# A gated mix of linear attention and a squared-relu block: TensorE in source order, keys of 448 columns, logits on VectorE

## The chip, the cores and the metric

The kernel runs on one core of a Trainium2 chip. The metric is the device time of one execution in microseconds (us); lower is better. A core has a matrix engine (TensorE, PE in the profile; its weight loads are PEld), three elementwise engines (VectorE = DVE, ScalarE = ACT, GpSimd = POOL), and SyncE (SP), which here issues nearly all DMAs. Each engine takes its own instructions in the order in which they stand in its queue, and waits on semaphores for the others.

## The reference

All tensors are fp32: 2048 tokens, model width 448, 16 heads of 28, hidden width 1792.

```python
def _A_ref(x, wqkv, wo):                       # linear attention
    q, k, v = split_heads(x @ wqkv)
    phi = lambda t: where(t > 0, t + 1, exp(t)) + 1e-6
    pq, pk = phi(q), phi(k)
    kv = einsum("bhsd,bhse->bhde", pk, v)
    z  = einsum("bhsd->bhd", pk)
    num = einsum("bhqd,bhde->bhqe", pq, kv)
    den = einsum("bhqd,bhd->bhq", pq, z)[..., None] + 1e-6
    return merge_heads(num / den) @ wo
def _B_ref(x, w1, b1, w2, b2):                 # squared relu block
    h = maximum(x @ w1 + b1, 0)
    return (h * h) @ w2 + b2
g = sigmoid((x * gate_w).sum(-1, keepdims=True))
out = g * _A_ref(x, ...) + (1 - g) * _B_ref(x, ...)
```

## The kernel before

Every fp32 operand of a product is split into a high and a low part of a rounded fp32 type; a product is then three matmuls (high × high, high × low, low × high). The width of 448 is cut into three chunks of 128 rows and a last one of 64, whose high and low parts share one chunk, so a full contraction over the width is 3 + 3 + 3 + 2 = 11 matmuls. The splits are elementwise work: ScalarE makes the high part (`split_hi`), VectorE the low part by a subtraction (`split_lo`); GpSimd takes a few.

The tokens are cut into four blocks `b` of 512, and the 1792 hidden columns into 14 tiles `f` of 128. The names in the profile:

- `up(b,f)`: 11 matmuls of 512 columns into `h_ps` (line 213). `hidden`: relu and square on ScalarE (`hr`, lines 217 and 218), then high and low part on VectorE (`hh`, `hl`). `down(b,f)`: 12 matmuls of 448 columns into the four `o_ps` tiles (line 242).
- `keys(t)`: 11 matmuls into `k_ps` for each of 16 token tiles `t`; 450 columns, since the gate's weights stand twice beside the 448 key columns, and a copy on VectorE (line 280) takes the logit from there. Then phi (`e`, `r`), the split (`ph`, `pl`), and `nh`, `nl`, the split of the raw `xn` tile.
- `gram(b,c)`: the products of keys and x, `g_ps`, summed in `gsum`.
- `kv_product`: `kv_ps`, then `kv_h`, `kv_l`. `m_product(j)`: for each of four groups of heads, three matmuls of the split `wo` (`woh`, `wol`) with kv into `m_ps`; ScalarE and VectorE evacuate it into the tile `m`, and five DMAs of GpSimd's queue bring it to `m_s`.
- `queries(b,c)`: `q_ps`, 11 matmuls (7 for c = 3). For c = 3 ScalarE copies the result (`qv`), eight small DMAs on SP swap its rows (`qr`), and VectorE adds the two (`join`). `after` is phi (exp on ScalarE, lines 261 and 262 on VectorE) and the sum `ds` for the denominators.
- `denominators(b)`: `d_ps`, from the split `dh`, `dl` of `ds`; VectorE makes `rec` from it. `scaled(b,c)`: the queries times `rec`, split (`qh`, `ql`). `attention(b,i)`: 11 matmuls of 448 columns with `m_s` (`a_ps`), added to `part`. `finish(b,i)`: the output tile, and its store.

Pass 1 goes through the four blocks with f = 0 to 6, and keeps the partial sums of `down` in `part`; the keys of a block and its `gram` go along. Pass 2 goes through the blocks in the order 3, 0, 1, 2 with f = 7 to 13; `kv_product` and `m_product` are in its first block, with the queries of block 3 between them, and in each block the queries of the next are made. PSUM has three pools: four tiles for `o_ps`, two for `h_ps`, and two (`ms_p`) shared by everything else: `k_ps`, `g_ps`, `kv_ps`, `m_ps`, `q_ps`, `d_ps`, `a_ps`, and two of the first four `h_ps` tiles. A new tile there waits until the one that had its bank has been read.

The order on every engine is set by a scheduler, which orders the program's instructions. Steps that read a result later are put on a list (`todo`), which `run_todo` empties a step on.

Of the kernel before, what the change touches and what calls it, by code (L numbers as in the profile page):

```python
# [7 lines left out]
F = mybir.dt.float32  # L8
# [22 lines left out]
def gated_mix_kernel(ctx: ExitStack, tc: tile.TileContext, xt, xn, wk, wq, wv, wo, w1a, w1b, w2, b1, b2, hmask,  # L31
# [4 lines left out]
    keep = ctx.enter_context(tc.tile_pool(name="keep", bufs=1))  # L36

# [122 lines left out]
    warm = keep.tile([P, 400], mybir.dt.bfloat16, name="warm")[:, :256]  # L160
# [42 lines left out]
    def up_chunk(ps, b, f, c):  # L203
        h, fl = divmod(f, NH)
        g, i = divmod(fl, 4)
        w, cols = w1_s[h, g], slice(i * P, (i + 1) * P)
        xh, xl = xs[b]
        if c < 3:
            terms = [(w[:, c, cols], xh[:, c]), (w[:, c, cols], xl[:, c]), (w[:, 4 + c, cols], xh[:, c])]
        else:  # L210
            terms = [(w[:, 3, cols], xh[:, 3]), (w[:, 3, cols], xl[:, 3])]
        for n, (a, m) in enumerate(terms):
            pe.matmul(ps, a, m, start=(c == 0 and n == 0), stop=(c == 3 and n == 1))  # L213

    def hidden(ps, b, f):
        r = slot([P, TB], F, f"hr{b}_{f}")
        act.activation(r, ps, AF.Relu, bias=b1_s[:, f:f + 1])  # L217
        act.activation(r, r, AF.Square)  # L218
        h = slot([P, TB], R, f"hh{b}_{f}")
        lo = slot([P, TB], R, f"hl{b}_{f}")  # L220
        split_hi(dve, h, r)
        split_lo(dve, lo, r, h)
        hs[f] = (h, lo)

    def up(b, f):
# [3 lines left out]
        hidden(ps, b, f)  # L229
# [34 lines left out]
    def keys(t):  # L264
        b, i = divmod(t, 4)
        ps = ms_p.tile([P, 512], F, name=f"k_ps{t}", tag="ms")
        products(ps[:, :D + 2], [term for c in range(4)
                                 for term in terms_x(*xs[b], slice(i * P, (i + 1) * P), wk_s, slice(0, D + 2), c)])
# [9 lines left out]
        def after():  # L278
            phi(ps[:, :D], e, r, p)
            dve.tensor_copy(logit[:, t:t + 1], ps[:, D:D + 1])  # L280
# [12 lines left out]
            pend[t] = (ph, pl, nh, nl)  # L293
# [19 lines left out]
    wq_s = keep.tile([P, 7, TB], R, name="wq_s")  # L313
# [72 lines left out]
    def m_product(j):  # L386
        wh, wl = wo_s.pop(j)
        ps = ms_p.tile([P, 512], F, name=f"m_ps{j}", tag="ms")
        products(ps[:, :D], [(kv[0][:, j], wh), (kv[0][:, j], wl), (kv[1][:, j], wh)])
        m = late.tile([P, 2, D], R, name=f"m{j}", tag="m", bufs=1)  # L390

        def after():
            split_hi(act, m[:, 0], ps[:, :D])
            split_lo(dve, m[:, 1], ps[:, :D], m[:, 0])

            p = j * 32
            for c in range(3):
                pool.dma_start(out=m_s[p:p + 32, c::4, :D][:, :2], in_=m[c * 32:c * 32 + 32])
            pool.dma_start(out=m_s[p:p + 16, 3, :D], in_=m[96:112, 0])
            pool.dma_start(out=m_s[p + 16:p + 32, 3, :D], in_=m[112:, 1])  # L400
        return [after]
# [4 lines left out]
    def queries(b, c):  # L406
# [25 lines left out]
        def swap():  # L432
# [4 lines left out]
            return [join]  # L437
# [30 lines left out]
    def attention(b, i):  # L468
# [13 lines left out]

    todo = []
# [10 lines left out]
    for c in range(4):  # L494
        if c == 0:
            split_x(0, 0, 0, TB // 2)
            split_w1(0, 0, 0, hi_eng=dve)
            split_x(0, 0, TB // 2, TB)
# [3 lines left out]
        for f in range(4):  # L502
            up_chunk(first[f], 0, f, c)
    for f in range(2):
        hidden(first[f], 0, f)
    split_w2(0)
    split_w2(1)
    for f in range(2, 4):
        hidden(first[f], 0, f)

    wkm = keep.tile([P, 3632], R, name="wk_s", tag="wkm", bufs=1)
    wk_s = wkm[:, :7 * TB].rearrange("p (c n) -> p c n", c=7)

    load_xn(0)
# [15 lines left out]
    for c in range(4):  # L530
        split_w1(0, 1, c)
# [25 lines left out]
    todo += gram(0, 0)  # L557
    split_x(1, 2)
    down(0, 5)
    run_todo()  # L560
    todo += gram(0, 1)
    split_x(1, 3)

    for b in range(1, NB):
        for f in range(NH):
            run_todo()
            up(b, f)
            if f == 0:
                down(b - 1, NH - 1)
                half_done(b - 1)  # L570
                if b == 1:
                    todo += gram(0, 2)
                    run_todo()
                    todo += gram(0, 3)
                    run_todo()
# [48 lines left out]
    for n, b in enumerate(order):  # L624
        then = order[n + 1] if n + 1 < NB else None
        for f in range(NF - NH, NF):
            fl = f - NH
            run_todo()
            up(b, f)
# [6 lines left out]
            else:  # L636
                down(order[n - 1], NF - 1)
                for i in range(4):
                    finish(order[n - 1], i)
            if n == 0:  # L640
                if fl < 4:
                    todo += queries(b, (3, 0, 1, 2)[fl])
                if fl == 0:
# [5 lines left out]
                    m_s = keep.tile([P, 3632], R, name="m_s", tag="wkm", bufs=1)  # L649
                    m_s = m_s[:, :7 * D].rearrange("p (c n) -> p c n", c=7)  # L650
                    for j in range(2):
                        load_wo(j)
                if fl == 1:
                    for c in range(4):
                        split_w1(1, 1, c)
                if fl in (1, 2):
                    for j in range(2 * fl - 2, 2 * fl):
                        split_wo(j)
                        todo += m_product(j)
                    if fl == 1:  # L660
                        for j in range(2, 4):
                            load_wo(j)
# [10 lines left out]
                if fl == 6:  # L673
                    for i in range(4):
                        attention(b, i)
            else:
                if fl == 0:
                    todo += denominators(b)
                if fl == 1:
                    for c in range(4):  # L680
                        scaled(b, c)
                if 2 <= fl < 6:
                    attention(b, fl - 2)
            if then is not None:
# [8 lines left out]
                if n == 0 and fl in (5, 6):  # L693
                    for c in ((3, 0), (1, 2))[fl - 5]:
# [57 lines left out]
```

## Time and profile before

| | |
|---|---|
| median of 3 runs | 442.16 us (442.0 to 442.78) |
| profiled execution | 441.92 us, span 440.1 |
| granted clock of TensorE | 1.000 |
| TensorE busy | 432.9 us (98%), 2054 matmuls |
| VectorE, ScalarE, GpSimd busy | 268.0 (61%), 172.7 (39%), 58.5 (13%) |

The span is what the profile records from first to last instruction. A row of groups gives busy time, then the mean of one in ns, then the engine's idle time ahead of them with what ended most of it (`<-`). A row of the timeline or of the chain begins with start and duration in us. Matmuls overlap: a record of 0.39 us follows the one before it by 0.23, so a start-to-start distance tells more than a duration.

### The profile page before, as it was taken

To read this page: it belongs to the slowest core of one execution; us is meant where nothing else is said; L and a number is where in the kernel's file an instruction comes from. 1 tells how busy PE (TensorE), PEld (TensorE's weight loads), DVE (VectorE), ACT (ScalarE), POOL (GpSimd) and SP (SyncE) were. 2 spreads that over 40 slices of the span, in tenths; PEclk is the share of its full clock that TensorE was granted. 3 is DMA by queue.
4 is the path that set the end of the run, shared out by engine and by line. 5 is a ranking of instruction groups with operands and counts; after the bars stand their busy time and mean duration, and the time that the engine had idled before them with its cause. 6 is when DMAs were issued, how large, how long until landed. Compare 5 with 4: busy or idle time off the path is not lost.

```text
span 440.1 us, 5482 instructions
## 1 busy us (share of the span) xinstructions
PE 432.9 (98%) x2054; PEld 380.7 (87%) x2054; DVE 268.0 (61%) x452; ACT 172.7 (39%) x298; POOL 58.5 (13%) x76
## 2 busy tenths in 40 slices
PE   9999999999999999999999989999999999999996
PEld 6798898899888889898988868888888898888895
DVE  5958436552587427573467668788454984549423
ACT  5955235331355114451344334335322453234321
POOL 0233124210252005420002420000000000000000
PEclk9999999999999999999999999999999999999999
DMA  7652201021031210333146311040100501002002
GB/s 264 188 174 69 89 13 57 24 66 47 24 118 31 67 45 1 110 102 82 54 123 151 73 38 24 1 147 33 25 0 0 181 0 26 0 0 85 1 1 83
DMA packets 18315, 28.77 MB, mean 65 GB/s; under 512 B 2880, under 2 KB 12784, under 8 KB 18288
## 3 DMA queue, kind: packets, MB, share of 16 engines
q1 hardware_dynamic: 17072, 26.81, 19.9%
q0 software_dynamic: 1216, 1.61, 1.9%
q8 instruction: 16, 0.26, 0.3%
q14 instruction: 11, 0.09, 0.1%
HBM read 22.09 MB, written 3.67 MB: 59 GB/s over the span
## 4 chain that ended last, share of the span: by engine, by line
PE 91%; DVE 3%; DMA 2%; ACT 2%; issue 1%; SPq 0%; DVEq 0%; ACTq 0%
PE o_ps L242 30%; PE h_ps L213 28%; PE q_ps L77 8%; PE a_ps L77 8%; PE g_ps L77 8%; PE k_ps L77 7%; DMA wkr<-in_wk 1%; DMA xr<-in_xt 1%; PE kv_ps L364 1%; ACT hr L217 1%; PE m_ps L77 1%; DVE wk_s L65 0%; DVE hh L62 0%; DVE r L261 0%; DVE r L262 0%
## 5 line engine op out<-in xcount | busy, mean ns | idle before, releaser
L213 PE MATMUL h_ps<-xh,w 128*128 128x512 f32 x392 | 126.9, 392 | 0.1
L242 PE MATMUL o_ps<-w,hh 128*128 128x448 f32 x448 | 125.5, 363 | 0.7 <-DVE hh L62 0.7
L242 PEld LDWEIGHTS o_ps<-w,hh 128*128 128x128 f32 x448 | 83.8, 188 | 10.2 <-DVE hh L62 1.4
L213 PE MATMUL h_ps<-xl,w 128*128 128x512 f32 x224 | 87.5, 391 | 0.0
L213 PEld LDWEIGHTS h_ps<-xh,w 128*128 128x128 f32 x392 | 73.5, 188 | 15.4 <-ACT xh L58 0.4
L242 PE MATMUL o_ps<-w,hl 128*128 128x448 f32 x224 | 79.6, 363 | 0.0
L217 ACT ACTIVATE hr<-h_ps,b_s 128x512 f32<-128x512 f32 x56 | 38.3, 683 | 96.9 <-PE h_ps L213 89.8
L62 DVE CAST hh<-hr 128x512 fp32r<-128x512 f32 x56 | 25.3, 452 | 40.4 <-ACT hr L218 40.0
L213 PEld LDWEIGHTS h_ps<-xl,w 128*128 128x128 f32 x224 | 42.1, 188 | 8.3 <-DVE xl L65 0.4
L242 PEld LDWEIGHTS o_ps<-w,hl 128*128 128x128 f32 x224 | 42.0, 188 | 2.9 <-DVE hl L65 0.2
L65 DVE TENSOR_TENSOR hl<-hr,hh 128x512 fp32r<-128x512 f32 x56 | 41.1, 734 | 2.2
L218 ACT ACTIVATE hr<-hr 128x512 f32<-128x512 f32 x56 | 35.3, 630 | 1.3
L77 PE MATMUL k_ps<-wk_s,xh 128*128 128x450 f32 x112 | 33.7, 367 | 0.0
L77 PE MATMUL q_ps<-xh,wq_s 128*128 128x512 f32 x100 | 33.0, 390 | 0.0
L77 PE MATMUL a_ps<-m_s,qh 128*128 128x448 f32 x112 | 32.2, 362 | 0.0
L65 POOL TENSOR_TENSOR nl<-xnr,nh 128x384 fp32r<-128x384 f32 x16 | 18.2, 1139 | 94.2 <-ACT nh L58 94.2
L286 POOL TENSOR_TENSOR ksum<-ksum,r 128x448 f32<-128x448 f32 x15 | 19.3, 1284 | 52.1 <-DVE r L262 52.1
L481 DVE SCALAR_TENSOR_TENSOR part<-part,gate,u 128x448 f32<-128x448 f32 x16 | 10.9, 683 | 24.9 <-ACT u L480 24.9
L480 ACT ACTIVATE u<-a_ps,gate 128x448 f32<-128x448 f32 x16 | 10.2, 635 | 37.2 <-PE a_ps L77 37.2
L261 DVE TENSOR_SCALAR r<-k_ps 128x448 f32<-128x448 f32 x16 | 10.0, 623 | 23.7 <-ACT e L260 21.7
L77 PE MATMUL k_ps<-wk_s,xl 128*128 128x450 f32 x64 | 23.6, 369 | 0.0
L77 PE MATMUL g_ps<-pl,nh 128*128 128x448 f32 x64 | 23.3, 364 | 0.3 <-DVE pl L65 0.3
(104 smaller groups left out, 562.0 us busy)
## 6 DMA issues: line engine op xcount, KB each, us to landing
xr<-in_xt SPq DMA_DIRECT2D x27, 256.0 KB, 3.2
xnr<-in_xn SPq DMA_DIRECT2D x16, 224.0 KB, 2.6
out<-out SPq DMA_DIRECT2D x16, 224.0 KB, 2.0
w2r<-in_w SPq DMA_DIRECT2D x14, 224.0 KB, 2.9
w1r<-in_w1a SPq DMA_DIRECT2D x8, 256.0 KB, 2.8
w1r<-in_w1b SPq DMA_DIRECT2D x8, 192.0 KB, 2.9
m_s<-m POOLq DMA_DIRECT2D x12, 112.0 KB, 2.7
wqr<-in_wq SPq DMA_DIRECT2D x4, 256.0 KB, 3.0
```

Of the source, the lines that this page charges most:

```text
L62: eng.tensor_copy(hi, src)
L65: eng.tensor_tensor(lo, src, f32(hi), op=ALU.subtract)
L77: pe.matmul(out_ps, a, b, start=(i == 0), stop=(i == n - 1))
L213: pe.matmul(ps, a, m, start=(c == 0 and n == 0), stop=(c == 3 and n == 1))
L217: act.activation(r, ps, AF.Relu, bias=b1_s[:, f:f + 1])
L218: act.activation(r, r, AF.Square)
L242: pe.matmul(o_ps[i][:, :D], a, m, start=(f % NH == 0 and n == 0), stop=(f % NH == NH - 1 and n == 2))
L261: dve.tensor_scalar(r, ps, 0.0, 1e-6, op0=ALU.max, op1=ALU.add)
L286: pool.tensor_tensor(ksum, ksum, p, op=ALU.add)
L364: pe.matmul(kv_ps[:JE, js], wv_s[c][:, js], gsum[c][:, js], start=(c == 0), stop=(c == 3))
L480: act.activation(u, ps[:, :D], AF.Copy, scale=gate[:, 0, t:t + 1])
L481: dve.scalar_tensor_tensor(part[t], part[t], gate[:, 1, t:t + 1], u, op0=ALU.mult, op1=ALU.add)
```

## The change

TensorE's instructions now keep the order of the source; the other engines are still ordered by the scheduler. The source is rearranged for it. In the head, x is loaded ahead of w1, and the first contraction runs term by term over four up tiles; 15 instead of 18 warming matmuls; wk is split ahead of the first hidden tiles, and w1's second group is loaded right behind wk and split between them. The first and the last hidden tile are made in halves (`parts`). Keys have 448 columns; the logit is a VectorE instruction over the raw `xn` tile and a broadcast copy of the gate's weights (`gw_s`), with an accumulated sum. `gram(0,·)` comes later, `m_product` is one per step, evacuated at once, `join` a step later, the attention of block 3 goes into the next block, `scaled` and `attention` of later blocks a step back.

```diff
-    for _ in range(18):
+    for _ in range(15):
...
+    for c in range(4):
+        load_w1(0, 1, c)
...
-        products(ps[:, :D + 2], [term for c in range(4)
-                                 for term in terms_x(*xs[b], slice(i * P, (i + 1) * P), wk_s, slice(0, D + 2), c)])
+        products(ps[:, :D], [term for c in range(4)
+                             for term in terms_x(*xs[b], slice(i * P, (i + 1) * P), wk_s, slice(0, D), c)])
...
-            dve.tensor_copy(logit[:, t:t + 1], ps[:, D:D + 1])
...
+            dve.scalar_tensor_tensor(e, raw, 1.0, gw_s, op0=ALU.mult, op1=ALU.mult, accum_out=logit[:, t:t + 1])
...
-        def after():
-            split_hi(act, m[:, 0], ps[:, :D])
-            split_lo(dve, m[:, 1], ps[:, :D], m[:, 0])
...
+        split_hi(act, m[:, 0], ps[:, :D])
+        split_lo(dve, m[:, 1], ps[:, :D], m[:, 0])
...
-            return [join]
+            return [lambda: [join]]
...
+    ctx.enter_context(tc.manual_schedule(engines={pe.engine}))
...
+        if c == 0:
+            for n in range(3):
+                for f in range(4):
+                    up_chunk(first[f], 0, f, c, n)
...
+    for c in range(4):
+        split_w(wk_s, c, wk_raw[c], act, dve)
+    hidden(first[0], 0, 0, 2)
+    hidden(first[1], 0, 1)
+    hidden(first[2], 0, 2)
+    for c in range(4):
+        split_w1(0, 1, c)
+    hidden(first[3], 0, 3)
...
-    todo += gram(0, 0)
     split_x(1, 2)
     down(0, 5)
-    run_todo()
-    todo += gram(0, 1)
+    todo += gram(0, 0)
...
-            up(b, f)
+            up(b, f, 2 if then is None and f == NF - 1 else 1)
...
+                    if n == 1:
+                        attention(order[0], i)
                     finish(order[n - 1], i)
             if n == 0:
+                if 1 <= fl < 5:
+                    m_product(fl - 1)
...
-                if fl in (1, 2):
-                    for j in range(2 * fl - 2, 2 * fl):
-                        split_wo(j)
-                        todo += m_product(j)
...
+                if 1 <= fl < 4:
+                    split_wo(fl)
...
-                if fl == 6:
-                    for i in range(4):
-                        attention(b, i)
...
-                if fl == 1:
-                    for c in range(4):
-                        scaled(b, c)
-                if 2 <= fl < 6:
-                    attention(b, fl - 2)
+                if 1 <= fl < 3:
+                    scaled(b, 2 * fl - 2)
+                    scaled(b, 2 * fl - 1)
+                if 3 <= fl:
+                    attention(b, fl - 3)
...
+    down(last, NF - 2, range(3))
     for i in range(4):
-        for f in (NF - 2, NF - 1):
-            down(last, f, [i])
+        if i == 3:
+            down(last, NF - 2, [i])
+        down(last, NF - 1, [i])
         finish(last, i)
```

How the instructions move is seen in the order of each engine's queue (name of the output, then the inputs; the numbers only tell tiles of one name apart). First ScalarE in the head, from the first hidden tile on; `h_ps0_2` is the third up tile, whose bank keys(0) takes. Before:

```order
L217 ACTIVATE hr0_0_231<-h_ps0_0_161,b1_s_115 128x512
L218 ACTIVATE hr0_0_231<-hr0_0_231 128x512
L217 ACTIVATE hr0_1_238<-h_ps0_1_162,b1_s_115 128x512
L218 ACTIVATE hr0_1_238<-hr0_1_238 128x512
L217 ACTIVATE hr0_2_251<-h_ps0_2_163,b1_s_115 128x512
```

Now:

```order
L233 ACTIVATE hr0_0_253<-h_ps0_0_168,b1_s_127 128x256 x2
L234 ACTIVATE hr0_0_253<-hr0_0_253 128x256 x2
L59 ACTIVATE w1_01_278<-w1r010_146 128x384
L233 ACTIVATE hr0_1_264<-h_ps0_1_169,b1_s_127 128x512
L59 ACTIVATE w1_01_278<-w1r011_148 128x384
L234 ACTIVATE hr0_1_264<-hr0_1_264 128x512
L59 ACTIVATE w1_01_278<-w1r012_150 128x384
L59 ACTIVATE w1_01_278<-w1r013_152 128x384
L233 ACTIVATE hr0_2_271<-h_ps0_2_170,b1_s_127 128x512
```

The four casts of w1's second group (`w1_01`) have moved ahead of the relu of the third up tile.

Second, ScalarE in the first block of pass 2, behind the evacuation of kv. Before:

```order
L58 ACTIVATE kv_h_2036<-kv_raw_2034 112x4x112
L434 COPY qv3_2008<-q_ps3_3_1998 128x512
L217 ACTIVATE hr3_8_2082<-h_ps3_8_2070,b1_s_115 128x512
L58 ACTIVATE w2_12_2152<-w2r12_2052 128x448
L218 ACTIVATE hr3_8_2082<-hr3_8_2082 128x512
L58 ACTIVATE xh0_2159<-xr0_0_2057 128x512
```

Now:

```order
L59 ACTIVATE kv_h_2040<-kv_raw_2038 112x4x112
L59 ACTIVATE woh0_2056<-wor0_2052 112x448
L59 ACTIVATE m0_2117<-m_ps0_2113 128x448
L446 COPY qv3_2012<-q_ps3_3_2002 128x512
L233 ACTIVATE hr3_8_2090<-h_ps3_8_2078,b1_s_127 128x512
L59 ACTIVATE w2_12_2158<-w2r12_2060 128x448
```

The copy of `qv3`, after which `q_ps3_3`'s bank is free, now stands behind the evacuation of the first m product. On TensorE the same place reads, before (in the middle of `up(3,9)`):

```order
L213 MATMUL h_ps3_9_2189<-xh3_1321,w1_10_1814 128x512 x2
L77 MATMUL m_ps0_2132<-woh0_2128,kv_h_2036 128x448
L213 MATMUL h_ps3_9_2189<-xl3_1322,w1_10_1814 128x512
L213 MATMUL h_ps3_9_2189<-xh3_1321,w1_10_1814 128x512 x2
L77 MATMUL m_ps0_2132<-wol0_2129,kv_h_2036 128x448
```

Now, behind `down(3,7)`:

```order
L256 MATMUL o_ps3_7_3_2109<-w2_7_1759,hl3_7_1981 128x448
L78 MATMUL m_ps0_2113<-woh0_2056,kv_h_2040 128x448
L78 MATMUL m_ps0_2113<-wol0_2057,kv_h_2040 128x448
L78 MATMUL m_ps0_2113<-woh0_2056,kv_l_2041 128x448
L78 MATMUL q_ps3_0_2125<-xh3_1325,wq_s_165 128x512
```

The three matmuls of an m product now stand together, and the next queries right behind them; so it is with all four.

Third, TensorE in pass 2, ahead of `down(1,8)` (`w2_8`). Before:

```order
L213 MATMUL h_ps1_10_3200<-xh1_2716,w1_10_1814 128x512
L213 MATMUL h_ps1_10_3200<-xl1_2717,w1_10_1814 128x512
L213 MATMUL h_ps1_10_3200<-xh1_2716,w1_10_1814 128x512 x2
L213 MATMUL h_ps1_10_3200<-xl1_2717,w1_10_1814 128x512
L213 MATMUL h_ps1_10_3200<-xh1_2716,w1_10_1814 128x512 x2
L213 MATMUL h_ps1_10_3200<-xl1_2717,w1_10_1814 128x512
L213 MATMUL h_ps1_10_3200<-xh1_2716,w1_10_1814 128x512 x2
L242 MATMUL o_ps1_7_0_3102<-w2_8_1825,hh1_8_3098 128x448 x2
```

Now:

```order
L225 MATMUL h_ps1_9_3142<-xl1_2710,w1_10_1818 128x512
L225 MATMUL h_ps1_9_3142<-xh1_2709,w1_10_1818 128x512 x2
L225 MATMUL h_ps1_9_3142<-xl1_2710,w1_10_1818 128x512
L256 MATMUL o_ps1_7_0_3106<-w2_8_1829,hh1_8_3100 128x448 x2
L256 MATMUL o_ps1_7_0_3106<-w2_8_1829,hl1_8_3101 128x448
```

Before, ten matmuls of `up(1,10)` stood between `up(1,9)` and `down(1,8)`; now none.

More of the change, by code (lines that the diff above doesn't have):

```diff
@@ L201, in gated_mix_kernel, with up_chunk @@
     hs = {}
-    def up_chunk(ps, b, f, c):
+    def up_chunk(ps, b, f, c, only=None):
         h, fl = divmod(f, NH)
@@ L212, in up_chunk, with hidden, up @@
         for n, (a, m) in enumerate(terms):
-            pe.matmul(ps, a, m, start=(c == 0 and n == 0), stop=(c == 3 and n == 1))
-    def hidden(ps, b, f):
+            if only in (None, n):
+                pe.matmul(ps, a, m, start=(c == 0 and n == 0), stop=(c == 3 and n == 1))
+    def hidden(ps, b, f, parts=1):
         r = slot([P, TB], F, f"hr{b}_{f}")
-        act.activation(r, ps, AF.Relu, bias=b1_s[:, f:f + 1])
-        act.activation(r, r, AF.Square)
         h = slot([P, TB], R, f"hh{b}_{f}")
         lo = slot([P, TB], R, f"hl{b}_{f}")
-        split_hi(dve, h, r)
-        split_lo(dve, lo, r, h)
+        for i in range(parts):
+            c = slice(i * TB // parts, (i + 1) * TB // parts)
+            act.activation(r[:, c], ps[:, c], AF.Relu, bias=b1_s[:, f:f + 1])
+            act.activation(r[:, c], r[:, c], AF.Square)
+            split_hi(dve, h[:, c], r[:, c])
+            split_lo(dve, lo[:, c], r[:, c], h[:, c])
         hs[f] = (h, lo)
-    def up(b, f):
+    def up(b, f, parts=1):
         ps = mm_p.tile([P, 512], F, name=f"h_ps{b}_{f}", tag="mm")
@@ L311, in gram @@
         return [after]
[L313 removed]
+    wq_s = keep.tile([P, 8 + 7 * TB], R, name="wq_s")[:, 8:]
+    wq_s = wq_s.rearrange("p (c n) -> p c n", c=7)
     wq_raw = {}
@@ L390, in m_product @@
         m = late.tile([P, 2, D], R, name=f"m{j}", tag="m", bufs=1)
-        def after():
-            split_hi(act, m[:, 0], ps[:, :D])
-            split_lo(dve, m[:, 1], ps[:, :D], m[:, 0])
[L396 to L401, printed above, removed]
+        split_hi(act, m[:, 0], ps[:, :D])
+        split_lo(dve, m[:, 1], ps[:, :D], m[:, 0])
+        p = j * 32
+        for c in range(3):
+            pool.dma_start(out=m_s[p:p + 32, c::4][:, :2], in_=m[c * 32:c * 32 + 32])
+        pool.dma_start(out=m_s[p:p + 16, 3], in_=m[96:112, 0])
+        pool.dma_start(out=m_s[p + 16:p + 32, 3], in_=m[112:, 1])
     pq, qs, den = {}, {}, {}
@@ L501, in gated_mix_kernel @@
             split_x(0, c)
[L502 to L505, printed above, removed]
+        if c == 0:
+            for n in range(3):
+                for f in range(4):
+                    up_chunk(first[f], 0, f, c, n)
+        else:
+            for f in range(4):
+                up_chunk(first[f], 0, f, c)
     split_w2(0)
     split_w2(1)
[L508 to L514, printed above, removed]
+    wk_s = keep.tile([P, 7, D], R, name="wk_s", tag="wkm", bufs=1)
+    for c in range(4):
[6 more added lines that the diff above has]
+    hidden(first[3], 0, 3)
     load_w2(2)
     load_w2(3)
-    for c in range(4):
-        split_w(wk_s[:, :, :D + 2], c, wk_raw[c], act, dve)
+    load_xn(0)
+    load_xn(1)
     down(0, 0)
-    load_xn(1)
-    for c in range(4):
-        load_w1(0, 1, c)
     todo += keys(0)
     split_w2(2)
+    load(gw_s, gw.partition_broadcast(P))
     load(b2_s, b2.partition_broadcast(P))
@@ L571, in gated_mix_kernel @@
                 if b == 1:
[L572 to L575, printed above, removed]
+                    for c in range(1, 4):
+                        todo += gram(0, c)
+                        run_todo()
             else:
```

97 lines of the change are left out of this document (52 added, 45 removed).

## The prediction

> **What bounds the kernel now.** I read the page first (busy shares, then the chain that ended last), then the longest wait of TensorE, then a table of stretches (here 50 to 205 us: its length, the busy time of TensorE, of its weight loads, of VectorE, ScalarE and GpSimd).
>
> ```profile
> span 440.1 us, 5482 instructions
> ...
> PE 432.9 (98%) x2054; PEld 380.7 (87%) x2054; DVE 268.0 (61%) x452; ACT 172.7 (39%) x298; POOL 58.5 (13%) x76
> ...
> PE 91%; DVE 3%; DMA 2%; ACT 2%; issue 1%; SPq 0%; DVEq 0%; ACTq 0%
> ```
>
> ```profile
> PE d_ps L77 <- ACT dh L58: 1.3, 1, 1.3
> ```
>
> ```profile
> 50.00:205.00 155.00, 155.00 (x740) 138.88 (x739) 83.52 (x138) 56.35 (x101) 36.23 (x39) 1.00 0.20 58
> ```
>
> TensorE is the bound: 98% of the span and 91% of the chain are its. In the table of windows it is busy for all of 50 to 205 us, nearly the whole of pass 1, so there is no hole there to win. A change can shorten the stream itself or close a handful of holes elsewhere, or open new ones. So I take the holes of before one by one, then look in the new order of instructions for places where TensorE waits for another queue. Times are worked out against the profiled execution (441.92 us: span 440.1 and 1.8 around it), which is 0.24 below the median of 442.16.
>
> **1. Keys of 448 columns.** From the chain of waits:
>
> ```profile
> 69.41 2.26 PE k_ps L77 x11
> 71.67 2.52 PE h_ps L213 x11
> ...
> 315.78 2.20 PE a_ps L77 x11
> ```
>
> ```profile
> L280 DVE COPY logit<-k_ps 128x1 f32<-128x1 f32 x16 | 2.4, 148 | 0.0
> ...
> L262 DVE SCALAR_TENSOR_TENSOR r<-e,r 128x448 f32<-128x448 f32 x16 | 11.4, 712 | 0.0
> ```
>
> Eleven matmuls of 450 columns take 2.26, eleven of 448 (attention) 2.20: 0.06 times 16 tiles is **−1.0 us**, all on TensorE. The Trainium skill, "TensorE: Matmul & The Clock Gate", section "Back-to-back issue gap", speaks against it: N/2.4 + 2.5 ns would make two columns 0.8 ns a matmul, an estimate of 0.15 us in all. The rows show 5 ns; by the page the sum below would be 0.8 us higher. I take the rows. The logit moves to VectorE as a 448-column scalar_tensor_tensor. None of that kind with an accumulated sum is in the trace; between the copy that it replaces (0.148) and the nearest row of its kind (0.712) I take the latter, 0.56 more per tile, 9 us in all. What hides it is VectorE's room in pass 1: by the window above it is busy 83.5 of 155 us. Without that cover it would cost up to 9; I take 0 and keep 0 to 0.5.
>
> **2. Head: up to keys(0).**
>
> ```profile
> 16.16 1.08 PE L242 MATMUL o_ps<-w,hh 128*128 128x448 f32 x4 [0.75 <-DVE hh L62]
> ...
> 18.89 0.56 PE L77 MATMUL k_ps<-wk_s,xh 128*128 128x450 f32 x2
> ```
>
> ```profile
> 14.09 0.69 ACT L217 ACTIVATE hr<-h_ps,b_s 128x512 f32<-128x512 f32 x1
> ...
> 219.00 1.75 ACT L58 ACTIVATE w<-w1r 128x384 fp32r<-128x384 f32 x4
> ```
>
> down(0,0) waits for VectorE, which has just finished the split of wk. That stays, so earlier first matmuls bring nothing; only a half hidden tile has to be cast (about 0.2 instead of 0.43), and down(0,0) starts near 15.95 instead of 16.16. It is 12 matmuls of 0.2, so TensorE wants keys(0) at 18.4. But keys(0) takes the PSUM bank of the third up tile, which ScalarE's relu of that tile frees. Before, that was ScalarE's third relu (third row of the order: relu, square, relu, square, relu). Now the four casts of w1 group 1 stand ahead of it: from about 14.3, two relus and two squares of half width (1.6 in all), the relu and square of the second tile (0.7 + 0.65) and four casts (1.75) end at 18.65 (19.0 by the durations, less some 0.35 where one starts before the last has ended), and the third relu near 19.35. Bounds: relu free at 18.4 (no wait) and 19.8. Before, keys(0) started at 18.89 with one matmul of down(0,1) behind it, like 18.7. So **+0.65** (−0.3 to +1.1).
>
> **3. gram(0,0).** It stood two steps too early:
>
> ```profile
> 46.70 0.56 PE L242 MATMUL o_ps<-w,hh 128*128 128x448 f32 x2
> 47.44 0.48 PE L77 MATMUL g_ps<-ph,nh 128*128 128x448 f32 x1 [0.18 <-ACT ph L58]
> ...
> 48.60 0.47 PE L77 MATMUL g_ps<-pl,nh 128*128 128x448 f32 x1 [0.28 <-DVE pl L65]
> ```
>
> Start to start against a step of 0.20, these two waits and the slow step behind each cost 0.34 + 0.12 + 0.44 + 0.11 = 1.0. In source order the group comes after all of down(0,5), when VectorE's split, done at 48.6, is past: **−1.0** (−1.0 to −0.5).
>
> **4. kv and the m products (pass 2, block 3).** Here the order decides.
>
> ```profile
> 227.41 2.41 PE o_ps L242 x12
> 229.82 2.52 PE q_ps L77 x11
> ...
> 236.07 0.63 PE m_ps L77 x3
> ```
>
> ```profile
> L434 ACT COPY qv<-q_ps 128x512 f32<-128x512 f32 x4 | 2.3, 584 | 5.5 <-PE q_ps L77 5.5
> ...
> L58 ACT ACTIVATE m<-m_ps 128x448 fp32r<-128x448 f32 x4 | 2.2, 543 | 4.8 <-PE m_ps L77 3.0 <-DMA m_s<-m 1.8
> ```
>
> ```profile
> L440 DVE TENSOR_TENSOR qv<-qv,qr 128x512 f32<-128x512 f32 x4 | 2.8, 689 | 0.4 <-DMA qr<-qv 0.3
> ...
> L65 DVE TENSOR_TENSOR m<-m_ps,m 128x448 fp32r<-128x448 f32 x4 | 2.5, 621 | 2.6 <-ACT m L58 2.6
> ...
> L261 DVE TENSOR_SCALAR qr<-qv 128x512 f32<-128x512 f32 x4 | 1.7, 426 | 0.1
> ```
>
> ```profile
> 226.64 5.69 SPq L51 DMA_DIRECT2D qr<-qv  x8
> ```
>
> ```profile
> xr<-in_xt SPq DMA_DIRECT2D x4, 256.0 KB, 4.7
> ...
> qr<-qv SPq DMA_DIRECT2D x8, 32.0 KB, 2.7
> ```
>
> First wait, q(3,0). m_product(0) now follows down(3,7) and ends at 229.8 + 0.63 = 230.45. q(3,0) needs the bank that ScalarE frees by copying qv; in ScalarE's new order that copy stands behind the evacuation of m0, which waits for m0. So 230.45 + 0.54 + 0.58 = 231.55: **+1.1** (1.0 to 1.3).
>
> Second wait, q(3,1). TensorE is at 231.55 + 2.52 (q) + 2.54 (up) + 2.41 (down) + 0.63 (m1) = 239.65. q(3,1) takes m1's bank, free after ScalarE's 0.54 and VectorE's 0.62: at least 1.2. Ahead of that VectorE instruction stands the qv addition, which waits for the eight swap copies. These start 5 us later than before (231.55 for 226.64); the last is issued after about 5.0 and lands 2.7 later, 239.3, then 0.69 + 0.43 + 0.62 with a little between: 241.2. **+1.6** (1.2 to 3.0, the upper end if the copies take the 4.7 of the xr loads).
>
> ```profile
> L65 DVE TENSOR_TENSOR hl<-hr,hh 128x512 fp32r<-128x512 f32 x56 | 41.1, 734 | 2.2
> L62 DVE CAST hh<-hr 128x512 fp32r<-128x512 f32 x56 | 25.3, 452 | 40.4 <-ACT hr L218 40.0
> ```
>
> Third, down(3,9). Behind the copies SP issues wor2, wor3, w2r13, xr0_2, xr0_3. The last goes out near 239.0, lands 4.7 later at 243.7; then ScalarE's sign split, relu and square (each like the relu row, 2.0 in all) and VectorE's cast and subtraction (0.45 and 0.73 by these rows), all queued in this order, give hh9 at 246.2 and hl9 at 246.9, where TensorE wants them at 246.35 and 246.75: **+0.4** (0 to 1.5).
>
> Fourth, the denominators.
>
> ```profile
> 254.89 0.60 ACT L260 ACTIVATE qe<-q_ps 128x512 f32<-128x512 f32 x1 [7.00 <-PE q_ps L77]
> ...
> 256.73 0.39 PE L213 MATMUL h_ps<-xl,w 128*128 128x512 f32 x1
> ...
> 258.42 0.69 DVE L65 TENSOR_TENSOR dl<-ds,dh 128x512 fp32r<-128x512 f32 x1 [0.70 <-ACT dh L58]
> ...
> 258.44 0.50 PE L77 MATMUL d_ps<-dh,hm 128*128 128x512 f32 x1 [1.32 <-ACT dh L58]
> ...
> 259.02 0.50 PE L213 MATMUL h_ps<-xh,w 128*128 128x512 f32 x1
> ```
>
> ```profile
> L451 DVE TENSOR_SCALAR rec<-d_ps 128x256 f32<-128x256 f32 x8 | 3.0, 416 | 0.0
> ```
>
> The old hole (1.71 and 0.58 for two steps of 0.23, 1.9 with the step behind) goes: after q(3,2) TensorE now has up, down and m3, 5.5 us, against 4.2 from exp to the end of the split of d (254.89 to 259.11): **−1.9** (−1.9 to −1.0). What is late next: the first queries of block 0 stand right behind d and take its bank, which VectorE frees by two rec instructions (0.42 each, 0.8 with overlap) that themselves queue behind hh11 and hl11: **+1.0** (0.8 to 1.3).
>
> **5. down(1,8) and down(2,8).** In pass 2 the scheduler had put matmuls of up(b,10) ahead of down(b,8), ten of the 11 in block 1; source order does not.
>
> ```profile
> 337.48 2.49 PE h_ps L213 x11
> ...
> 342.38 0.47 PE d_ps L77 x2
> ```
>
> ```profile
> 350.63 0.69 DVE L65 TENSOR_TENSOR hl<-hr,hh 128x512 fp32r<-128x512 f32 x1
> ```
>
> Block 1: q2 ends at 337.48. VectorE's instructions from there to hl8 are the same in the same order, so hl8 is ready at 351.32 again. TensorE has up7, down13, d, up8, down7, up9: 3 × 2.49 + 2 × 2.41 + 0.47 = 12.76, and the third matmul of down8 comes 0.4 later, at 350.65: a wait of 0.7. The same in block 2: **+1.4** (0.5 to 2.0). Block 0 has attention(3,·) in that place and no wait.
>
> **6. Tail.**
>
> ```profile
> 433.12 1.14 PE L242 MATMUL o_ps<-w,hh 128*128 128x448 f32 x4
> ```
>
> The fourth of these waits for the last hidden tile; with the last hidden tile in halves and products of f = 12 ahead of it that goes: **−0.2** (−0.3 to 0).
>
> **Sum.** −1.0 + 0.65 − 1.0 + (1.1 + 1.6 + 0.4 − 1.9 + 1.0) + 1.4 − 0.2 = +2.05. The profiled execution would be 444.0, the median 444.2 (0.5% slower). With every term at its lower end it is −1.0, at its upper end near +8.
>
> **The rivals.** A: the m products do not stop TensorE. If ScalarE's queue were not held by m0's evacuation, or something of 1.2 us stood between each product and the queries behind it, the first, second, third and the rec wait (4.1) fall away: 440.1, faster. For it: before, the same products cost TensorE no wait at all. Against: then up tiles stood around them, now nothing does. B: the swap copies land late. If they and the x loads behind them get in each other's way, q(3,1) and down(3,9) stand at their upper ends, +2.5: 446.7. For it is the 4.7 of the x loads in the same stretch; against, the 2.7 median of the copies. C: no difference. An up tile takes 2.52 at 71.67 and 2.49 at 337.48; if source order takes that 0.03 from all 56, 1.7 us come back: 442.5. Against it: in pass 1 the groups stood in order before, too.
>
> **How the numbers follow.** Forecast 0.48 (its own range 442.9 to 445.6), A 0.22, B 0.12, C 0.18. About 0.2% is what can be told from no change here, so 441.3 to 443.0 is "same": C. Faster is A, 0.22; slower the forecast and B, 0.60. The range runs from A to B, 439.8 to 446.8, and leaves out what is beyond the two.
>
> **What would show it.** In the waits of TensorE after: k_ps on ACT hr near 1; q_ps on ACT qv near 1.1; q_ps on DVE m at 1.2 to 3; q_ps on DVE rec near 1; o_ps on DVE hl twice near 0.7; none of d_ps in block 3, none of g_ps; k_ps rows of 2.20. Wrong would be the forecast if the q_ps waits are missing, or if pass 1 shows waits for VectorE, which now carries the logits.

## The result, and the profile after

The changed kernel takes 447.61 us (median of 6 runs, 446.88 to 451.23), the kernel before 442.08 on the same chip (6 runs, 441.96 to 442.78). The ratio is 1.0126, with a 95% interval of 1.0102 to 1.015: slower by 5.5 us, where 2.05 was forecast. The profiled execution took 448.06 us with a span of 446.3, so 6.2 longer in span than before.

The page's first line, the busy shares and the chain that ended last, after:

```profile
span 446.3 us, 5506 instructions
...
PE 433.3 (97%) x2051; PEld 379.6 (85%) x2051; DVE 282.9 (63%) x473; ACT 171.9 (39%) x301; POOL 63.6 (14%) x76
...
PE 87%; DVE 4%; DMA 4%; ACT 2%; SPq 1%; issue 1%; DVEq 0%; ACTq 0%
```

TensorE's work is not longer, but its share of the chain has fallen from 91 to 87%. What came in is in the list of its waits (us in total, times, longest):

```profile
PE o_ps L256 <- DVE hh L63: 1.7, 3, 1.2
PE o_ps L256 <- DVE hl L66: 1.6, 3, 0.5
PE q_ps L78 <- DVE m L66: 1.3, 1, 1.3
PE q_ps L78 <- ACT qv L446: 1.1, 1, 1.1
PE warm_ps L173 <- DVE part L170: 1.1, 1, 1.1
PE q_ps L78 <- DVE rec L463: 0.9, 1, 0.9
PE h_ps L225 <- DVE xl L66: 0.7, 1, 0.7
PE k_ps L78 <- ACT hr L233: 0.6, 1, 0.6
```

No `d_ps` and no `g_ps` wait is left, as forecast; five of the rows are the forecast's waits (the two of `q_ps` on `m` and `qv`, `rec`, `k_ps`, `o_ps` on `hl`). The first row was to be small, and the `h_ps` row, at 6.7 us in the head, had no term. The chain of waits shows it (start and duration):

```profile
228.45 0.63 PE m_ps L78 x3
...
229.10 0.54 ACT m L59
229.65 0.48 ACT qv L446
...
235.38 1.96 DMA qr<-qv
...
237.61 0.49 DVE qv L452
238.10 5.48 DMA xr<-in_xt
...
245.75 0.43 DVE hh L63
...
246.28 0.70 DVE hl L66
...
247.02 2.28 PE o_ps L256 x10
```

m0 is evacuated, then `qv` is copied, then the eight swap copies go out one by one on SP, and the last x load of the next block is queued behind them. It is issued at 238.10 and lands 5.48 later; ScalarE and VectorE split it ahead of the hidden tile that `down(3,9)` wants. TensorE's own rows there:

```profile
244.67 0.39 PE L225 MATMUL h_ps<-xl,w 128*128 128x512 f32 x1
246.23 0.68 PE L256 MATMUL o_ps<-w,hh 128*128 128x448 f32 x2 [1.17 <-DVE hh L63]
247.02 0.47 PE L256 MATMUL o_ps<-w,hl 128*128 128x448 f32 x1
247.33 0.57 PE L256 MATMUL o_ps<-w,hh 128*128 128x448 f32 x2
```

The wait in the bracket is not all: from 244.67 the next matmul starts 1.56 later, the next two take 0.79 to 247.02, and then one takes 0.31, against steps of 0.23 once and 0.20 otherwise: the place costs 1.33 + 0.39 + 0.11 = 1.83.

One wait of this kind was not foreseen at all. In the third block of pass 2 (block 1) a chain of the same kind runs into `down(1,9)`:

```profile
349.68 5.03 DMA xr<-in_xt
...
354.72 0.63 ACT xh L59
...
359.34 0.61 DVE hl L66
...
360.00 2.08 PE o_ps L256 x9
```

The x loads stand behind the four stores in both kernels. The issue times of the four loads there (ns, least, median and most), before and after:

```profile
L51 SPq DMA_DIRECT2D xr<-in_xt x4: 339/390/422, 346.4 to 347.8; - x4
```

```profile
L52 SPq DMA_DIRECT2D xr<-in_xt x4: 373/381/1594, 349.2 to 351.8; - x4
```

The first goes out 2.8 us later, of which 2.6 are the delay of the whole stream up to here (the queries ahead end 2.6 later); but one of the four took SP 1.59 us.

### The profile page after: what moved, and what is told of

The parts are those of the page before. It is cut to its first block, busy times and chain, and to the rows that moved or that the text cites. A ratio compares the mean times of both kernels' runs of the same rounds, so it can differ in the third digit from the quotient of the medians.

```text
span 446.3 us, 5506 instructions
## 1 busy us (share of the span) xinstructions
PE 433.3 (97%) x2051; PEld 379.6 (85%) x2051; DVE 282.9 (63%) x473; ACT 171.9 (39%) x301; POOL 63.6 (14%) x76
## 3 DMA queue, kind: packets, MB, share of 16 engines
q1 hardware_dynamic: 17216, 27.04, 19.6%
## 4 chain that ended last, share of the span: by engine, by line
PE 87%; DVE 4%; DMA 4%; ACT 2%; SPq 1%; issue 1%; DVEq 0%; ACTq 0%
PE o_ps L256 27%; PE h_ps L225 27%; PE k_ps L78 8%; PE g_ps L78 8%; PE a_ps L78 8%; PE q_ps L78 7%; DMA xr<-in_xt 2%; SPq L52 1%; DMA w1r<-in_w1a 1%; DVE rec L465 1%; ACT hr L233 1%; PE kv_ps L379 1%; DVE out L266 1%; DVE hl L66 1%; DMA qr<-qv 0%
## 5 line engine op out<-in xcount | busy, mean ns | idle before, releaser
L256 PE MATMUL o_ps<-w,hl 128*128 128x448 f32 x224 | 81.9, 366 | 1.7 <-DVE hl L66 1.6
L233 ACT ACTIVATE hr<-h_ps,b_s 128x512 f32<-128x512 f32 (+1 forms) x58 | 38.5, 668 | 98.3 <-PE h_ps L225 87.6
L63 DVE CAST hh<-hr 128x512 fp32r<-128x512 f32 (+1 forms) x58 | 26.2, 452 | 40.0 <-ACT hr L234 39.9
L66 DVE TENSOR_TENSOR hl<-hr,hh 128x512 fp32r<-128x512 f32 (+1 forms) x58 | 40.5, 699 | 2.2
L234 ACT ACTIVATE hr<-hr 128x512 f32<-128x512 f32 (+1 forms) x58 | 35.5, 615 | 1.3
L78 PE MATMUL k_ps<-wk_s,xh 128*128 128x448 f32 x112 | 32.8, 363 | 0.6 <-ACT hr L233 0.6
L66 POOL TENSOR_TENSOR nl<-xnr,nh 128x384 fp32r<-128x384 f32 x16 | 19.5, 1219 | 74.2 <-ACT nh L59 74.1
L299 POOL TENSOR_TENSOR ksum<-ksum,r 128x448 f32<-128x448 f32 x15 | 22.8, 1518 | 43.7 <-DVE r L276 38.3
L78 PEld LDWEIGHTS q_ps<-xh,wq_s 128*128 128x128 f32 x100 | 18.8, 188 | 8.1 <-DVE m L66 1.7
L78 PE MATMUL q_ps<-xl,wq_s 128*128 128x512 f32 x60 | 23.5, 391 | 0.0
```

The lines of the kernel that those rows point to most:

```text
L63: eng.tensor_copy(hi, src)
L66: eng.tensor_tensor(lo, src, f32(hi), op=ALU.subtract)
L78: pe.matmul(out_ps, a, b, start=(i == 0), stop=(i == n - 1))
L233: act.activation(r[:, c], ps[:, c], AF.Relu, bias=b1_s[:, f:f + 1])
L234: act.activation(r[:, c], r[:, c], AF.Square)
L256: pe.matmul(o_ps[i][:, :D], a, m, start=(f % NH == 0 and n == 0), stop=(f % NH == NH - 1 and n == 2))
```

## The experiments

Each ran beside the kernel before, whose median was 442.33 to 442.49. Ratios are to it. The changed kernel's 447.61 is the other yardstick.

**The order alone (e1_sched).** The changed source, ordered by the scheduler on TensorE too.

```diff
-    ctx.enter_context(tc.manual_schedule(engines={pe.engine}))
```

> The changed kernel with TensorE ordered by the scheduler again; everything else of the change is kept. Theory (the loss is TensorE standing in source order in front of results that other queues deliver late): matmuls of up tiles fill the holes, the two q_ps waits and those of down(1,8), down(1,9), down(2,8) shrink, 440 to 443 us. Rival (the other engines' orders and the loads are what is late, whoever orders TensorE): 446 us or more, with the same waits.

Measured: 440.1 us, ratio 0.9928 (0.9907 to 0.9949), faster than the kernel before. The waits of TensorE that are left, beside the 1.1 at the very start:

```profile
PE q_ps L78 <- DVE m L66: 0.8, 1, 0.8
PE h_ps L225 <- DVE xl L66: 0.7, 1, 0.7
PE o_ps L256 <- DVE hh L63: 0.2, 1, 0.2
```

So one line costs 7.5 us, and all else in the change, ordered by the scheduler, is worth 2.3 in the other direction.

**The m products ahead of `down` (e2_m_first).**

```diff
             up(b, f, 2 if then is None and f == NF - 1 else 1)
+            if n == 0 and 1 <= fl < 5:
+                m_product(fl - 1)
...
-                if 1 <= fl < 5:
-                    m_product(fl - 1)
```

> The changed kernel with each m product ahead of the down tile of its step instead of behind it, so that 2.4 us of down stand between an m product and the queries that take the bank. Theory: the q_ps waits on ACT qv (1.1 by the waits of the changed kernel) and on DVE m (1.3) go, the swap copies start 2.4 us earlier, and with them the wait of down(3,9) (1.2 and more) goes or shrinks: 442.5 to 444.5 us. Rival (the wait only moves): TensorE comes earlier to down(3,9) and waits there instead; 446.5 to 447.6 us.

Measured: 446.34, ratio 1.007 (1.0045 to 1.0094). The `qv` wait is gone, and of the `m` wait 0.3 is left at q(3,1). But `q_ps` now waits 1.0 for `m` behind `d`, and the third product waits itself, for `woh` and then for `wol`, which VectorE makes behind the late x load; the clock then fell. From the waits, and a table of stretches (the length, busy time of TensorE, of its weight loads, of VectorE, ScalarE and GpSimd, and then the granted clock):

```profile
PE q_ps L78 <- DVE m L66: 1.3, 2, 1.0
...
PE m_ps L78 <- DVE wol L66: 1.0, 1, 1.0
PE m_ps L78 <- ACT woh L59: 0.6, 1, 0.6
...
245.00:249.00 4.00, 4.00 (x14) 3.60 (x13) 4.00 (x8) 1.53 (x3) 0.50 (x1) 0.57 0.04 7
```

The 12 matmuls of the `down` there took 3.97 instead of 2.41 us. The median stands nearer to the rival: a wait moved is not a wait removed where the same late load stands behind it. But not all of it is waits. The three of the eight runs with a mean granted clock of 0.999 to 1.000 took 444.26 to 445.35 us, the quickest of them inside the theory's 442.5 to 444.5, and the five with 0.992 to 0.996 took 446.16 to 448.36.

**Other banks in the head (e4_banks).** The first two up tiles take the shared pool's banks, so that `keys(0)` takes the first tile's.

```diff
-    first = [(mm_p if f < 2 else ms_p).tile(...)
+    first = [(ms_p if f < 2 else mm_p).tile(...)
```

> The changed kernel with the four first up tiles in the other PSUM pools: the first two in the shared pool, the last two in that of the up tiles, so that keys(0) takes the bank of the first tile. Theory: the wait of keys(0) for ScalarE's third relu (0.6 in the view of waits, 0.84 start to start) goes: 446.6 to 446.9 us. Rival: down(0,1) behind it then waits for its hidden tile, and the time stays at 447.6.

Measured: 445.6, ratio 1.0058 (1.0035 to 1.008). The wait of `k_ps` on `hr` is gone (0.84 start to start). The rest of the 2 us is elsewhere: in this profile the wait at `down(1,9)` was missing as well, since none of the x loads was held back, and `down(3,9)` cost 1.50 and not 1.83.

**The keys alone (e5_keys_only).** The kernel before, with keys of 448 columns, the logit on VectorE, and nothing else.

```diff
-            dve.tensor_copy(logit[:, t:t + 1], ps[:, D:D + 1])
...
+            dve.scalar_tensor_tensor(e, raw, 1.0, gw_s, op0=ALU.mult, op1=ALU.mult, accum_out=logit[:, t:t + 1])
...
-    wkm = keep.tile([P, 3632], R, name="wk_s", tag="wkm", bufs=1)
+    wkm = keep.tile([P, 3152], R, name="wk_s", tag="wkm", bufs=1)
```

> The kernel before with only the keys changed: 448 columns, the logit on VectorE over the raw tile. Theory: 16 times 0.06 less on TensorE and no new wait in pass 1: 0.9 to 1.0 us less than before, 441.1 to 441.3 us. By the Trainium skill's price per column (TensorE: Matmul & The Clock Gate, Back-to-back issue gap) it would be 0.15 less, an estimate. Rival (9 us more on VectorE are felt): 442 us or more, with waits of TensorE for VectorE in pass 1.

Measured: 443.9, ratio 1.0026 (1.0013 to 1.0039): slower by 1.5, not faster by 0.9. The keys did run in 2.20. Against it stand longer waits ahead of `gram(0,0)` (0.2 and 0.3 before; 0.9 more start to start), a wait of 0.8 for a split of x in the head (keys(0) starts 0.5 later), up tiles that take up to 2.56, and 0.4 behind the last matmul (see the table of the steps):

```profile
PE h_ps L214 <- ACT xh L58: 0.8, 1, 0.8
PE g_ps L77 <- DVE pl L65: 0.7, 1, 0.7
PE g_ps L77 <- ACT ph L58: 0.6, 1, 0.6
```

```profile
L290 DVE SCALAR_TENSOR_TENSOR e<-xnr,gw_s 128x448 f32<-128x448 f32 x16 | 14.2, 886 | 0.5
```

```profile
84.83 2.20 PE k_ps L77 x11
...
94.39 2.56 PE h_ps L214 x11
```

The logit takes 0.89, not 0.71, and is not free where a group of `gram` stands close behind. The up tiles are taken up again below; this run, too, has the tile of 3152 columns, so its loss is not that of the logit alone.

**An up tile ahead of `down` (e3_up_ahead).** In the third and fourth block of pass 2, which are blocks 1 and 2 (not block 0, as the expectation has it).

```diff
-            up(b, f, 2 if then is None and f == NF - 1 else 1)
+            ahead = n >= 2 and fl >= 2
+            for g in ([f, f + 1] if ahead and fl == 2 else [f + 1] if ahead and f + 1 < NF else [] if ahead else [f]):
+                up(b, g, 2 if then is None and g == NF - 1 else 1)
```

> The changed kernel, but in blocks 0, 1 and 2 of pass 2 TensorE takes the next up tile, up(b,f+1), ahead of down(b,f-1) from the third step on, so that each hidden tile gets about 5 us more before it is contracted. Theory: down(1,8), down(1,9) and down(2,8) wait only because in source order nothing but one up tile stands between the queries and them; the three waits (1.0, 1.0 and 1.4 us start to start) go: 447.6 - 3.2 = 444.4, with no new wait over 0.3. Rival: the vector engines are late there by more than one tile's worth, so the waits move to the attention products or to a later down and the time stays at 447 to 448.

Measured: 444.65, ratio 1.0058 (1.0036 to 1.0081), 3.0 less than the changed kernel. The three waits are gone, and none came in their place; of `o_ps` this row is left, and stands in the head and at `down(3,9)`, which in this profile cost 0.96 and not 1.83 although the edit does not touch that block:

```profile
PE o_ps L256 <- DVE hh L63: 0.5, 2, 0.3
```

**The swap copies on another queue (e9_swap_pool).**

```diff
-                load(r[p:p + 16], v[p ^ 16:(p ^ 16) + 16])
+                pool.dma_start(out=r[p:p + 16], in_=v[p ^ 16:(p ^ 16) + 16])
```

> The changed kernel, but the eight small copies that swap the rows of qv are issued on GpSimd's queue and not on SyncE's, so that the x loads behind them leave 4 to 5 us sooner. Theory: down(3,9) waits (1.8 us) because the x load of block 0 is issued behind the copies and lands 5.5 us later, and ScalarE and VectorE split it ahead of the hidden tile; with the copies out of that queue the wait goes: 447.6 - 1.8 = 445.8, waits of o_ps on DVE hh and hl in the first block of pass 2 near 0. Rival: the chain of elementwise work behind the two queries' waits is what is late, not the load; then down(3,9) still waits over 1 us and the time is 447 or more. If the copies on GpSimd's queue collide with the copies of the m products there, q(3,1) waits longer (over 1.6 us start to start).

Measured: 444.55, ratio 1.0044 (1.0028 to 1.006): 3.1 less than the changed kernel, not 1.8. `down(3,9)` no longer waits, and neither does q(3,1), which had waited 1.56 for the addition behind the copies. In the chain m1, q(3,1), up and `down(3,9)` follow one another without a gap:

```profile
237.87 0.62 PE m_ps L78 x3
238.49 2.51 PE q_ps L78 x11
241.00 2.49 PE h_ps L225 x11
243.50 2.41 PE o_ps L256 x12
```

GpSimd's queue holds the copies without harm to m; the `rec` wait grew from 0.9 to 1.2.

**The x loads ahead of the stores (e6_x_first).** From the second block of pass 2 on.

```diff
             else:
+                if then is not None:
+                    load_x(then, 0)
+                    load_x(then, 1)
                 down(order[n - 1], NF - 1)
...
-                if fl < 2:
+                if fl < 2 and (n == 0 or fl == 1):
```

> The changed kernel, but from the second block of pass 2 on the x loads of the next block are issued ahead of the stores of the finished one, not behind them. Theory: down(1,9) waits (1.0 us start to start in the profile) only because these loads leave 3 us later than before, one of them held back, and ScalarE and VectorE then split them ahead of the hidden tile; with the loads ahead that wait goes, down(1,8) and (2,8) stay: 447.6 - 1.0 = 446.6, and the spread of the runs shrinks. Rival: the wait is that of the queries' chain on VectorE, late by itself; then nothing changes: 447 to 448.

Measured: 447.27, ratio 1.0095 (1.0075 to 1.0116): 0.3 below the changed kernel, which is within the spread of the runs, and not 1.0. In its profile the wait at `down(1,9)` is gone, and the last x load ahead of `down(3,9)` took 6.03 instead of 5.48 and cost 0.84 more. But the wait is missing in the profiles of e2_m_first, e4_banks and e9_swap_pool too, where the loads stand behind the stores as in the changed kernel: in all of these VectorE starts on `hl` for `down(1,9)` 18.2 to 18.3 us after the last of the queries' matmuls, and in the changed kernel's profile 19.6. What is 1.4 late there is the one load that SP was slow to issue, so the theory of this run, that its place behind the stores is the cause, is not borne out. Why SP was held is open.

**Source order with every wait moved away (e11_all).** The edits of e2, e3, e4 and e9, and the denominators of block 3 a step later:

```diff
+            if n == 0 and fl == 5:
+                for step in denominators(b):
+                    step()
...
-                if fl == 4:
-                    todo += denominators(b)
```

> The changed kernel, in source order on TensorE, with every wait that was found moved away by hand: the m products ahead of down, up tiles ahead of down in later blocks of pass 2, the first two up tiles in the other pool's banks, the swap copies on GpSimd's queue, and the denominators of block 3 a step later, executed at once. Theory: it is not the source order as such that costs, but what stands late in it: the waits of 0.9 (keys(0)), 1.4 + 1.6 (queries), 1.8 (down(3,9)), 1.2 (rec) and 3.2 (down(1,8), (1,9), (2,8)) sum to 10 us; with most gone, 439 to 441, as with the scheduler. Rival: each closed hole reopens behind the next late queue, as it did when the m products alone were moved (446.3); then 443 to 446 and TensorE's waits still sum to over 5 us.

Measured: 438.6, ratio 0.9915 (0.9894 to 0.9937). Its waits, beside the 1.1 at the very start:

```profile
PE h_ps L225 <- DVE w L63: 0.3, 1, 0.3
PE h_ps L225 <- DVE xl L66: 0.2, 1, 0.2
PE o_ps L256 <- DVE hh L63: 0.2, 1, 0.2
```

So source order can be as fast as the scheduler; it is what stood late in it that cost 9 us.

**The scheduler with the swap moved (e10_sched_swap), and with all of it (e13_all_sched).** e1 with the edit of e9; e11 without the line of e1.

> The changed kernel with TensorE ordered by the scheduler again (440.1 us measured for that alone) and the eight swap copies on GpSimd's queue. Theory: that order has only 0.8 us of waits left behind the swap (q_ps on DVE m) and 0.2 at down(3,9), so the two edits add to at most -1.0: 439.1 to 440.1. Rival: the copies on GpSimd's queue delay the five copies of m there, and the attention of block 3 waits: 441 or more.

> The kernel in source order with all waits closed by hand (438.6 us measured), but with TensorE ordered by the scheduler. Theory: the order is worth nothing by itself where nothing stands late, so the time stays within 0.5 of 438.6. Rival: the scheduler does better with any source than a hand-written order does: 437.5 or less.

Measured: 438.39, ratio 0.9905 (0.9886 to 0.9924), and 437.93, ratio 0.9898 (0.9884 to 0.9912). e10 gained 1.7 on e1 where at most 1.0 was expected, and e13 lies 0.7 below e11, between its theory (within 0.5) and its rival (437.5). With nothing late the two orders are within 0.7 us. e13_all_sched has the lowest median of all, 1.0% under the kernel before; from e10 and e11 it can't be told apart by the intervals.

**Keys of 450 columns again (e12_keys_450), and 64 bytes (e14_shift).** e10, first with the logit copied from 450-column keys as before, then with 448 columns and only the tile of the split wk wider:

```diff
-    wk_s = keep.tile([P, 7, D], R, name="wk_s", tag="wkm", bufs=1)
+    wkm = keep.tile([P, 3152], R, name="wk_s", tag="wkm", bufs=1)
+    wk_s = wkm[:, :7 * D].rearrange("p (c n) -> p c n", c=7)
```

> The kernel with TensorE ordered by the scheduler and the swap copies on GpSimd's queue (438.4 us measured), but with keys of 450 columns again and the logit copied from there. Theory: with the keys and their grams far enough apart the 448 columns are a gain of 16 x 0.06 = 0.9 us there, so taking them back gives 439.3. Rival: as in the kernel before, where they alone cost 1.5 us, the logit on VectorE costs as much as the columns save; then 437.5 to 438.5.

> The kernel with TensorE ordered by the scheduler and the swap copies on GpSimd's queue (438.4 us measured), with one difference: the tile of the split wk (later of m) is 3152 columns wide and not 3136, so that every tile laid out behind it lies 64 bytes further on. No instruction, order or size of a matmul differs. Theory: the 450-column variant lost 1.7 of its 2.6 us because all up tiles ran 2.53 instead of 2.50, and that comes from where their operands lie: 438.4 + 1.7 = 440.1, h_ps rows of 2.51 to 2.57 in the chain. Rival: it comes from the 450-column keys or the copy of the logit themselves, then 438.4 and rows of 2.49 to 2.52.

Measured: 441.01, ratio 0.9966 (0.9953 to 0.9978), 2.6 above e10 and not 0.9; and 440.45, ratio 0.9957 (0.9943 to 0.9971), 2.1 above e10 with the same instructions in the same order on the engines. The chain in pass 1, first of e10, then of e14:

```profile
70.29 2.49 PE h_ps L225 x11
...
84.49 2.49 PE h_ps L225 x11
...
91.79 2.52 PE h_ps L225 x11
```

```profile
72.53 2.49 PE h_ps L225 x11
...
86.73 2.57 PE h_ps L225 x11
...
94.11 2.56 PE h_ps L225 x11
```

The mean start-to-start step of an up matmul away from waits is 227.6 ns in e10 and the changed kernel, 228.5 in the kernel before, 229.7 in e5, and 230.4 in e12 and e14. The last three are the runs whose tile has 3152 columns; it has 3136 in the changed kernel and e10, and 3632 in the kernel before. Times 616 matmuls, 2.8 ns are 1.7 us of e14's 2.1. (e14's profiled execution took 442.39 us, with the first `down` 2.0 later than in e10; its other four runs took 440.38 to 440.64, so the comparison uses the median.) The keys' step in e12 is 204.0 ns against 199.8 in e14: 0.74 us of its 2.6.

## Why the prediction was off

The sign held, and so did most of the mechanisms; the sum was 3.4 us short. Against its steps, start to start in the two profiles:

| step | forecast | measured |
|---|---|---|
| 1 keys, 176 matmuls | −1.0 | −0.9 |
| 2 head up to keys(0) | +0.65 | +0.9 |
| 3 gram(0,0) | −1.0 | −1.0 |
| 4 q(3,0) | +1.1 | +1.4 |
| 4 q(3,1) | +1.6 | +1.6 |
| 4 down(3,9) | +0.4 | +1.8 |
| 4 d | −1.9 | −1.9 |
| 4 rec | +1.0 | +1.2 |
| 5 down(1,8), down(2,8) | +1.4 | +2.4 |
| down(1,9), in the profiled execution | none | +1.0 |
| 6 tail | −0.2 | −0.25 |
| up tiles (rival C) | 0 | −0.5 |
| behind the last matmul | none | +0.4 |
| sum | +2.05 | +6.15 (span +6.15) |

The last term is not the kernel's own work. From the end of the last matmul to the end of the span it is 3.55 us before and 3.97 now, though the last store lands 2.65 after that matmul in both: behind that landing seven more of SyncE's closing semaphore waits now stand, 0.06 each. e5 has the 3.97 as well, and the runs with the copies on GpSimd's queue have 4.33 to 4.37.

Three steps failed, and the 0.4 behind the last matmul had no term. The first is `down(3,9)`. The forecast had the last x load issued at 239.0 and landed 4.7 later, but in before's clock. The terms ahead of it make the stream reach this place some 1.4 earlier (q(3,0) follows a product that starts at 228.45; by the forecast's clock it would start at 229.8). In that clock the load was issued 0.45 later than forecast (0.2 of it by the end of the eight swap copies, one of which held SP 1.38 us, and 0.3 in the five issues behind them), and landed after 5.48. That makes 1.2 of the 1.4. The 4.7 was a median of four loads, and the longest of them, 5.29, was this very load in the kernel before; nothing bound the new one to the median. (The 0.4 itself does not come out of the forecast's times either, by which `hl` was 0.15 late.)

In four profiles every engine has the same instructions in the same order from `kv_product` to this place, and the price goes with the landing:

| run | last x load, issue to landing | `down(3,9)` costs |
|---|---|---|
| e3_up_ahead | 4.79 | 0.96 |
| e4_banks | 5.14 | 1.50 |
| the changed kernel | 5.48 | 1.83 |
| e6_x_first | 6.03 | 2.67 |

The first and the last of these loads, in the chains of their runs:

```profile
237.78 4.79 DMA xr<-in_xt
```

```profile
238.32 6.03 DMA xr<-in_xt
```

So the term was a spread of about 1.0 to 2.7, and the forecast's 0 to 1.5 was too low. This is half of rival B: the x load was late, but the copies were not (q(3,1) cost the 1.6 of the forecast). e9 shows the dependence from the other side: with the copies off SP's queue the load leaves 4.5 us sooner, and q(3,1) and `down(3,9)` go through. What makes the landing vary is open.

The second is `down(1,9)`, for which step 5 had no term. It priced the loss of the ten matmuls of `up(1,10)` at `down(1,8)` only, but the tile behind it lost the same lead. Before, VectorE started on this `hl` 20.6 us after the last of the queries' matmuls and TensorE did not wait; in the changed kernel it did so after 19.6 and TensorE waited, and where no load was held back (18.2) the lead was just enough. So this term is no fixed price: it is 0 to 1.0, by the loads, and the runs around 447 may not have it.

The third is small and stands in every wait: the matmuls next to a stop are slow. `down(1,8)` waits 0.69 longer than a step for `hl`, just the forecast's 0.7, but the steps around it, 0.36, 0.31 and 0.31 in place of 0.23, 0.20 and 0.20, bring it to 1.04. In `down(2,8)` VectorE was also 0.4 later with `hh`, since a `qe` ahead of it had itself waited. Step 3 and the old hole in step 4 had counted the slow step with their waits; the new waits of steps 2, 4 and 5 had not.

Rival A (the products don't stop TensorE) fell: both waits came, 1.4 and 1.6 for a forecast of 1.1 and 1.6. Its condition was right, though: with the waits moved away (e11) the kernel is faster than before. Rival C said that source order would make up tiles 0.03 shorter. They are shorter by 0.01 in the mean (227.6 ns a matmul for 228.5), but the cause is not the order: e1, ordered by the scheduler, has 227.9, and e14 loses 1.7 us by a shift of tiles alone.

By the rule of the Trainium skill, "TensorE: Matmul & The Clock Gate", section "Back-to-back issue gap", N/2.4 + 2.5 ns for an isolated matmul, two more columns would be 0.8 ns, an estimate. This does not hold here: 450 columns cost 4.2 ns a matmul more than 448 in e12 and 5 in the kernel before, so step 1 was right to take the rows.

Step 1's cover held in the changed kernel, where `gram(0,0)` stands behind all of `down(0,5)`: no `g_ps` wait. e5 shows the price without it: the waits ahead of `gram(0,0)` are 0.9 longer there than before.

## What to carry to other kernels

Before an engine is pinned to source order, follow each wait in it back over every queue to its DMA, ask what stands there ahead of it, and cost a load at the longest landing nearby, not at the median. Where matmuls that stood ahead of a tile move away, look at the tiles behind it as well: they lose the same lead. Compare a change of tile sizes with a control that only moves the tiles.

## What the runs showed of the hardware

A shift of 64 bytes in where tiles lie, with no instruction changed, made the 11 matmuls of many up tiles take 2.56 to 2.57 instead of 2.49 to 2.52 us and the kernel 2.1 us slower (e14). Which operand's position it is was not tried.

After two stops of 0.6 and 1.0 us within 3 us (e2) TensorE's granted clock stood at 0.57 over 4 us, and a `down` took 3.97 us instead of 2.41. That the stops brought it on is not shown: in e6 a stop of 2.0 us at `down(3,9)` brought no such loss (1.00 over the 7 us from 245 on). The changed kernel's longest run, 451.23 us, has a mean granted clock of 0.996, the other five 0.998 to 0.999, so part of its spread goes with the clock; 0.003 of 449 us is 1.3 us, an estimate.

The last load of 256 KB of x behind the swap copies on SP took 4.79 to 6.03 us to land in the changed kernel, e3, e4 and e6, where the median of the 28 in the changed kernel is 3.4.

In block 3 of pass 2 one of the eight swap copies held SP 1.18 to 1.72 us in the changed kernel and in e1, e2, e3, e4 and e6, where the others take 0.57 to 0.61. In e9, with the copies on GpSimd's queue, no issue on SP took over 0.9. The cause is open.
